# Loading the first inputs in other pieces, turning `gate_w` on TensorE, and warm-up products on constants

## The chip, the cores and the metric

The kernel runs on one core of one Trainium2 chip. The metric is the device time of one execution in microseconds (us); lower is better. Several executions of the kernel before were timed, and one execution was recorded by the hardware profiler; all durations of single instructions below come from that one recorded execution.

## The reference

With x of 2048 tokens by 512 features, the reference adds two branches, mixed token by token by a gate:

```python
g = sigmoid((x * gate_w).sum(-1, keepdims=True))      # one number per token
a = A(x, wq, wk, wv, wo, beta)                        # attention in 4 segments of 512 tokens, 32 heads of 16
b = (gelu(x @ w_gate) * (x @ w_up)) @ w_down          # 1792 hidden features
out = g * a + (1 - g) * b
```

`A` is causal softmax attention inside each segment of 512 tokens, mixed per head (by `sigmoid(beta)`) with a linear-attention memory that is carried from segment to segment, and then a product with `wo`. All inputs and the output are bf16.

## The kernel before

**Layout.** A segment's x is held transposed, features on partitions: `xS[s]` is 128 partitions by 4 feature blocks (`fc`) by 512 tokens. K and Q are computed transposed (`u_k`, `u_q`: four products of 128 by 128 by 512 accumulate over `fc` in one PSUM bank, then a copy, called a cast in this text, brings them to SBUF). V is computed with tokens on partitions (`u_v`, four products of 448 columns for each of four token blocks `kt`). The last 64 columns of V and the gate's sum, `x @ gate_w`, come together in `u_vz` (tile `zT`): `gate_w` is kept as a further column, number 512, of the tile `wv`. `u_vz` reads columns 448 to 512, `u_v` reads columns 0 to 447.

**The start.** Everything is emitted in program order, engine by engine, and each engine runs its own list in that order. `load_inputs` (L134) issues seven transfers on SP's queue: x of segment 0 (into `x0`, which borrows the tile `G[1]`), `wk`, `wq`, `beta`, `wv`, `gate_w`, and `wga` (the weights of the gelu branch's gate product, 1.8 MB). x of segment 0 comes in as it lies in memory, 128 tokens by 512 features for each of four blocks, so every piece that one transfer row moves has 1 KB. Meanwhile `warm_up` (L155) clears a piece of `G[1]` on VectorE and runs six products of 512 columns and sixteen small ones on it; their results are not used. `transpose_x0` (L169) then turns x on TensorE, 16 products in four groups of four, one group per feature block, and VectorE and ScalarE copy the groups alternately to `xS[0]`. Then come, in this order on TensorE: three K blocks (`u_k(0, c)` for c below 3, tile `kT`), four Q blocks (`qT`), four V blocks (`vT`), `u_vz` (`zT`), and fourteen gate blocks (`u_gate`, tile `gT`, L440), which need `wga`. Between Q and V, `load_rest` (L143) has VectorE write a few elements of `xS[1]`; the transfer of x of segment 1 waits for that, and the other large weights (`wup`, `wdn`, `wo`) follow it in SP's queue.

**PSUM.** The tiles of the start (`warm`, `x0T`, `kT`, `qT`, `vT`, `zT`, `gT`) all take turns in the same four banks, tag `gen`. A tile can be written when the tile four before it has been read out.

**The rest.** After the fourteenth gate block a list scheduler, run when the program is built, has fixed one order of instructions for attention (`lg`, `pT`, `od`), memory, gate, up, down and output products of all four segments. It works with estimated costs (`MM512`, `EVAC`, `EXP_T` and so on) and does not look at the start, so this order is the same whatever the start does.

Of the kernel before, what the change touches and what calls it, by code (L numbers as in the profile page):

```python
# [13 lines left out]
P = 128  # L14
D = 512
# [3 lines left out]
DFF = 1792  # L19
FC = D // P  # L20
# [11 lines left out]
BF = dt.bfloat16  # L32
# [21 lines left out]
def kernel(  # L54
# [15 lines left out]
    nc = tc.nc  # L70
    S = A_x.shape[1]
    L = S // NSEG
    KT = L // P
    assert A_x.shape[0] == 1 and A_x.shape[2] == D and L == 512 and KT == 4
    x2 = A_x[0]
# [6 lines left out]
    pgen = ctx.enter_context(tc.tile_pool(name="pgen", bufs=4, space=bass.MemoryType.PSUM))  # L82

    def const(shape, dtype, name):
        return cpool.tile(shape, dtype, name=name, tag=name)

    xS = [const([P, FC, L], BF, f"x{i}") for i in range(NX)]
    wq = const([P, FC, D], BF, "wq")
    wk = const([P, FC, D], BF, "wk")
    wv = const([P, FC, D + 2], BF, "wv")  # L90
    wo = const([P, FC, D], BF, "wo")
    wup = const([P, FC, DFF], BF, "wup")
    wga = const([P, FC, DFF], BF, "wga")
    wdn = const([P, HS, D], BF, "wdn")
    ident = const([P, P], BF, "ident")
# [11 lines left out]
    G = [const([P, HS, L], BF, f"G{i}") for i in range(NG)]  # L107
# [17 lines left out]
    def gen(name):  # L125
        return pgen.tile([P, 512], F32, name=name, tag="gen")

    def x_seg(s):
        nc.sync.dma_start_transpose(xS[s % NX][:, :, :], x2[s * L:(s + 1) * L, :])

    def cols(dst, src):
        nc.sync.dma_start(dst[:, :, :], src.rearrange("(fc p) n -> p fc n", p=P))

    def load_inputs():  # L134
        nc.sync.dma_start(x0, x2[0:L, :].rearrange("(k p) d -> p k d", p=P))
        cols(wk, A_wk)
        cols(wq, A_wq)
        nc.sync.dma_start(beta[:, :], A_beta.rearrange("(o n) -> o n", o=1).to_broadcast((P, H)))
        cols(wv[:, :, 0:D], A_wv)
        nc.sync.dma_start(wv[:, :, D:D + 1], gate_w.rearrange("(fc p o) -> p fc o", p=P, o=1))  # L140
        cols(wga, B_w_gate)

    def load_rest():  # L143
        nc.vector.memset(xS[1][:, 0, 0:2], 0.0)
        x_seg(1)
        cols(wup, B_w_up)
        x_seg(2)
        cols(wdn, B_w_down)
        cols(wo, A_wo)


    x0 = G[1][:, 0:KT, :]
    zero = G[1][:, KT, :]

    def warm_up():  # L155
        nc.vector.memset(zero, 0.0)
        T = gen("warm")
        for i in range(6):
            nc.tensor.matmul(T[:, :], lhsT=zero[:, 0:P], rhs=zero, start=True, stop=True)

        U = gen("warm")
        for i in range(16):
            j, r = i // 2 % 4, i % 2
            nc.tensor.matmul((T, U)[r][32 * j:32 * j + 32, 0:256],
                             lhsT=zero[64 * r:64 * r + 64, 32 * j:32 * j + 32],
                             rhs=zero[64 * r:64 * r + 64, 0:256], start=True, stop=True,
                             tile_position=(64 * r, 32 * j))

    def transpose_x0():  # L169
        for fc in range(FC):  # L170
            T = pgen.tile([P, 1024], BF, name="x0T", tag="gen")
            for kt in range(KT):
                nc.tensor.transpose(T[:, kt * P:(kt + 1) * P],
                                    x0[:, kt, fc * P:(fc + 1) * P], ident[:, :])
            if fc % 2 == 0:
                nc.vector.tensor_copy(xS[0][:, fc, :], T[:, 0:512])
            else:
                nc.scalar.copy(xS[0][:, fc, :], T[:, 0:512])

    def setup_consts():  # L180
        nc.gpsimd.memset(bm[:, :, :], 1.0)
# [80 lines left out]
    def u_q(s, c):  # L262
        def f():
            T = gen("qT")
            for fc in range(FC):
                nc.tensor.matmul(T[:, :], lhsT=wq[:, fc, c * P:(c + 1) * P],  # L266
                                 rhs=xS[s % NX][:, fc, :],
                                 start=(fc == 0), stop=(fc == FC - 1))
                if fc < FC - 1:
                    yield MM512  # L270
            cast(QT[:, c, :], T[:, :])
            return MM512
        return 4 * MM512, EVAC, f
# [103 lines left out]
    def u_v(s, kt):  # L377
        def f():
            T = gen("vT")
            for fc in range(FC):  # L380
                nc.tensor.matmul(T[:, 0:DV], lhsT=xS[s % NX][:, fc, :][:, kt * P:(kt + 1) * P],  # L381
                                 rhs=wv[:, fc, 0:DV], start=(fc == 0), stop=(fc == FC - 1))
                if fc < FC - 1:
                    yield MM448
            cast(Vh[s % 2][:, kt, :, 0:HV // 2, 0:16].rearrange("q p h d -> q h p d"),
                 T[:, 0:DV].rearrange("q (h p d) -> q h p d", h=HV // 2, p=2))
            return MM448
        return 4 * MM448, EVAC, f
# [261 lines left out]

    ctx.enter_context(tc.manual_schedule())
    load_inputs()
    make_identity(nc, ident[:, :])
    warm_up()
    transpose_x0()
    setup_consts()

# [88 lines left out]
    def run(u):  # L746
        if u[0] == 0.0:
            u[2]()
        else:
            for _ in u[2]():  # L750
                pass
# [3 lines left out]
    for c in range(NC8):  # L755
        run(u_q(0, c))
    load_rest()
    for kt in range(KT):
        run(u_v(0, kt))
    run(u_vz(0))  # L760
# [182 lines left out]
    for pieces in visits:  # L943
# [17 lines left out]
        if lumps and lumps[0][0] == clock[0]:  # L961
            i = lumps.pop(0)[1]
# [5 lines left out]
        n = len(visits) - clock[0]  # L968
# [174 lines left out]
```

## Time and profile before

| | |
|---|---|
| median of 3 runs | 271.45 us (271.13 to 272.18) |
| profiled execution | 270.92 us, of which the span from first to last instruction is 269.2 us |
| TensorE (PE) busy | 262.6 us, 98% of the span |
| first warm-up product | 1.32 us after the start of the span |
| first transposing product | 4.79 us |
| first K product | 6.29 us |
| first gate product | 16.04 us |

Times in the views count from the start of the span. PE is TensorE's products, PEld its weight loads, DVE is VectorE, ACT ScalarE, POOL GpSimd, SP the engine whose queue issues the transfers (SPq is that issuing). A row of the timeline or of the chain gives start, duration, engine, line of the kernel, operation, and output tile `<-` input tiles; in brackets stands how long the engine sat idle before it and what ended that. An `xN` is the number of instructions merged into the row. A row of the windows gives for each engine the busy time in that stretch and the instructions, then the granted TensorE clock, the busy share of the 16 DMA engines, and GB/s. A row of the transfers gives KB and the time from issue to landing.

### The profile page before, as it was taken

The page shows a single profiled execution, that of the slowest core. Times are in us where ns is not written, and L with a number is a line of the kernel's source. Part 1 is how long each engine was busy: PE and PEld are TensorE (multiplying, and loading weights), DVE is VectorE, ACT ScalarE, POOL GpSimd, SP SyncE. Part 2 cuts the span into 40 slices and gives each one's busy share as a digit, 9 for nine tenths or more (in the row PEclk, how much of TensorE's full clock was granted, in tenths as well). Part 3 has the DMA queues.
Part 4 walks back from the last instruction along what each step waited for, and adds up shares of the span by engine and source line. Part 5 has one row for each costly group of instructions (what it writes and reads, how often), then busy time and mean ns, then how long its engine had stood idle before and what let it go on. Part 6 is the DMA issues. An engine that isn't in the chain of part 4 may idle for free.

```text
span 269.2 us, 6568 instructions
## 1 busy us (share of the span) xinstructions
PE 262.6 (98%) x2713; PEld 117.7 (44%) x2713; DVE 203.4 (76%) x390; ACT 208.8 (78%) x163; POOL 156.8 (58%) x298
## 2 busy tenths in 40 slices
PE   7999999999999999999999999999999999999993
PEld 2454434344454444545444444444444544344451
DVE  1899575968778787697986979596888588697374
ACT  3236889999997998889999988889888987567420
POOL 4000158897905979987811998596875079654400
PEclk9999999999999999999999999999999999999998
DMA  6899931200160000301042001100000300003102
GB/s 226 281 223 280 319 86 39 41 4 0 22 142 2 0 22 22 78 2 43 0 62 62 2 21 45 38 29 13 19 23 21 67 2 19 16 5 41 39 22 85
DMA packets 29986, 16.60 MB, mean 62 GB/s; under 512 B 20480, under 2 KB 28928, under 8 KB 29952
## 3 DMA queue, kind: packets, MB, share of 16 engines
q1 hardware_dynamic: 29952, 16.14, 23.6%
q8 instruction: 22, 0.36, 0.6%
q14 instruction: 12, 0.10, 0.1%
HBM read 8.14 MB, written 2.10 MB: 38 GB/s over the span
## 4 chain that ended last, share of the span: by engine, by line
PE 86%; POOL 5%; issue 4%; DMA 2%; ACT 1%; DVE 0%; SPq 0%; ACTq 0%; DVEq 0%; POOLq 0%
PE gT L440 19%; PE uT L461 17%; PE dT L477 14%; PE lg L602 8%; PE od L627 6%; PE aT L494 5%; PE qT L266 5%; PE kT L352 5%; PE vT L381 4%; POOL pT L611 3%; POOL KTm L362 2%; DMA wk<-in_A_wk_dram 2%; PE MT L515 1%; PE mn L584 1%; ACT pT L607 1%
## 5 line engine op out<-in xcount | busy, mean ns | idle before, releaser
L611 POOL TENSOR_SCALAR_AFFINE_SELECT pT<-pT 64x256 bf16<-64x256 bf16 x256 | 113.8, 445 | 94.6 <-ACT pT L607 81.7
L607 ACT ACTIVATE pT<-lg 128x2048 bf16<-128x2048 f32 x72 | 135.1, 1876 | 24.9 <-PE lg L602 21.6
L461 PE MATMUL uT<-x,wup 128*128 128x512 bf16 x224 | 60.4, 380 | 0.0
L440 PE MATMUL gT<-x,wga 128*128 128x512 bf16 x224 | 57.0, 380 | 0.0
L477 PE MATMUL dT<-wdn,G 128*128 128x512 bf16 x224 | 52.9, 380 | 0.0
L467 DVE TENSOR_TENSOR G<-uT,G 128x512 bf16<-128x512 f32 x56 | 38.1, 684 | 6.4 <-PE uT L461 6.2
L362 POOL TENSOR_SCALAR KTm<-ktb,eo 128x512 bf16<-128x512 bf16 x26 | 40.6, 1571 | 1.3
L634 DVE STREAM_TRANSPOSE oq<-od 128x512 f32<-128x512 f32 x32 | 21.0, 695 | 19.5 <-PE od L627 19.5
L477 PEld LDWEIGHTS <-G 128*128 128x128 bf16 x224 | 20.8, 98 | 25.0 <-issue 2.1
L440 PEld LDWEIGHTS <-wga 128*128 128x128 bf16 x224 | 20.4, 98 | 24.0 <-issue 2.2
L461 PEld LDWEIGHTS <-wup 128*128 128x128 bf16 x224 | 19.8, 98 | 24.0 <-issue 5.4
L602 PE MATMUL lg<-QT,KTm 32*128 32x192 bf16 (+7 forms) x512 | 28.6, 287 | 0.0
L289 DVE CAST G<-gT 128x512 bf16<-128x512 f32 x24 | 16.5, 688 | 9.9 <-PE gT L440 9.7
L602 PEld LDWEIGHTS <-KTm 32*128 32x128 bf16 x512 | 8.3, 92 | 28.4 <-issue 28.0
L627 PE MATMUL od<-pT,V 64*32 64x128 bf16 (+7 forms) x512 | 19.4, 284 | 0.2 <-POOL pT L611 0.2
L627 PE MATMUL od<-pT,Vs 64*32 64x128 bf16 (+7 forms) x512 | 19.4, 284 | 0.0
L455 ACT ACTIVATE G<-G 128x3584 bf16<-128x3584 bf16 x6 | 18.8, 3182 | 0.0
L640 DVE SCALAR_TENSOR_TENSOR o<-oq,ogs,rden 128x256 bf16<-128x256 f32 x32 | 17.0, 532 | 1.1
L352 PE MATMUL kT<-x,wk 128*128 128x512 bf16 x64 | 16.8, 380 | 0.4 <-DMA wk<-in_A_wk_dram 0.4
L266 PE MATMUL qT<-x,wq 128*128 128x512 bf16 x64 | 16.6, 379 | 0.0
L499 DVE SCALAR_TENSOR_TENSOR tB<-aT,gct,tB 128x512 bf16<-128x512 f32 x16 | 11.9, 746 | 6.0 <-PE aT L494 5.7
L494 PE MATMUL aT<-wo,oT 128*128 128x512 bf16 x64 | 16.5, 380 | 0.0
(94 smaller groups left out, 274.5 us busy)
## 6 DMA issues: line engine op xcount, KB each, us to landing
out_dram<-tB SPq DMA_DIRECT2D x16, 128.0 KB, 1.7
wga<-in_B_w_gate_dram SPq DMA_DIRECT2D x1, 1792.0 KB, 12.0
wup<-in_B_w_up_dram SPq DMA_DIRECT2D x1, 1792.0 KB, 9.9
wdn<-in_B_w_down_dram SPq DMA_DIRECT2D x1, 1792.0 KB, 8.0
Vs<-V SPq DMA_DIRECT2D x8, 144.0 KB, 2.6
G<-in_A_x_dram SPq DMA_DIRECT2D x1, 512.0 KB, 4.0
wk<-in_A_wk_dram SPq DMA_DIRECT2D x1, 512.0 KB, 4.9
wq<-in_A_wq_dram SPq DMA_DIRECT2D x1, 512.0 KB, 5.8
```

Source lines behind the costliest of these rows:

```text
L266: nc.tensor.matmul(T[:, :], lhsT=wq[:, fc, c * P:(c + 1) * P], rhs=xS[s % NX][:, fc, :], start=(fc == 0), stop=(fc == FC - 1))
L352: nc.tensor.matmul(T[:, :], lhsT=wk[:, fc, c * P:(c + 1) * P], rhs=xS[s % NX][:, fc, :], start=(fc == 0), stop=(fc == FC - 1))
L362: eng.tensor_scalar(out=KTm[:, (NC8 * s + c) % NK, :, p, :], in0=ktb[:, c, :].rearrange("q (b k) -> q b k", b=NB), scalar1=eo[:, p:p + 1], ...
L440: nc.tensor.matmul(T[:, :], lhsT=wga[:, fc, hs * P:(hs + 1) * P], rhs=xS[s % NX][:, fc, :], start=(fc == 0), stop=(fc == FC - 1))
L461: nc.tensor.matmul(T[:, :], lhsT=wup[:, fc, hs * P:(hs + 1) * P], rhs=xS[s % NX][:, fc, :], start=(fc == 0), stop=(fc == FC - 1))
L467: nc.vector.tensor_tensor(out=g, in0=T[:, :], in1=g, op=ALU.mult)
L477: nc.tensor.matmul(T[:, :], lhsT=G[s % NG][:, hs, qt * P:(qt + 1) * P], rhs=wdn[:, hs, :], start=(hs == 0), stop=(hs == HS - 1))
L494: nc.tensor.matmul(T[:, :], lhsT=oT[:, fc, qt * P:(qt + 1) * P], rhs=wo[:, fc, :], start=(fc == 0), stop=(fc == FC - 1))
L602: nc.tensor.matmul(lg[:, j, off:off + n], lhsT=KTm[rows, i % NK, b].rearrange("r p k -> r (p k)"), rhs=QT[rows, i % NC8, 64 * b:L], start= ...
L607: nc.scalar.activation(pT[:, :, :], lg[:, :, :], AF.Exp, scale=DH ** -0.5)
L611: nc.gpsimd.affine_select(out=v, in_=v, pattern=[[0, 4], [1, 64]], compare_op=ALU.is_ge, fill=0.0, base=0, channel_multiplier=-1)
L627: nc.tensor.matmul(od[p][32 * j:32 * j + 32, 64 * b:L], lhsT=w[:, 18 * h:18 * h + 32], rhs=t[rows, j, off:off + n], start=(b == 0), stop=( ...
```

## The change

x of segment 0 is loaded in two transfers of 256 tokens. In each of them a partition takes two neighbouring tokens, 2 KB in one piece; the transposed copy then puts token 2p+k of the half to its place, so that its writes step over every second element. `transpose_x0` goes half by half, each half in two groups that hold two feature blocks; VectorE copies the first group of each half, ScalarE the second. `wk` comes in two transfers of 256 columns, so its pieces are 512 bytes. `gate_w` comes as four rows of 128 elements into a corner of `G[1]`; a product with the identity turns them between Q and V (`transpose_gw`, in a PSUM bank of its own), and VectorE writes column 512 of `wv` from it. `beta` is issued after `wv`. `wga` comes in two transfers, 512 columns and 1280 columns. The warm-up products read constants that the preamble has set, one of them repeated by a step of zero, so the clearing on VectorE goes; five large products remain of six.

```diff
     def load_inputs():
-        nc.sync.dma_start(x0, x2[0:L, :].rearrange("(k p) d -> p k d", p=P))
-        cols(wk, A_wk)
+        half = L // 2
+        for i in range(2):
+            nc.sync.dma_start(x0[:, 2 * i:2 * i + 2, :],
+                              x2[half * i:half * (i + 1), :].rearrange("(p k) d -> p k d", p=P))
+        for i in range(2):
+            n = slice(D // 2 * i, D // 2 * (i + 1))
+            cols(wk[:, :, n], A_wk[:, n])
         cols(wq, A_wq)
+        nc.sync.dma_start(gw4, gate_w.rearrange("(fc p) -> fc p", p=P))
+        cols(wv[:, :, 0:D], A_wv)
         nc.sync.dma_start(beta[:, :], A_beta.rearrange("(o n) -> o n", o=1).to_broadcast((P, H)))
-        cols(wv[:, :, 0:D], A_wv)
-        nc.sync.dma_start(wv[:, :, D:D + 1], gate_w.rearrange("(fc p o) -> p fc o", p=P, o=1))
-        cols(wga, B_w_gate)
+        for n in (slice(0, 4 * P), slice(4 * P, DFF)):
+            cols(wga[:, :, n], B_w_gate[:, n])
...
     x0 = G[1][:, 0:KT, :]
-    zero = G[1][:, KT, :]
+    gw4 = G[1][0:FC, KT, 0:P]
 
     def warm_up():
-        nc.vector.memset(zero, 0.0)
         T = gen("warm")
-        for i in range(6):
-            nc.tensor.matmul(T[:, :], lhsT=zero[:, 0:P], rhs=zero, start=True, stop=True)
+        for i in range(5):
+            nc.tensor.matmul(T[:, :], lhsT=nc.const_aps.tensor(1.0, [P, P], BF),
+                             rhs=nc.const_aps.tensor(1.0, [P, 512], BF), start=True, stop=True)
...
             nc.tensor.matmul((T, U)[r][32 * j:32 * j + 32, 0:256],
-                             lhsT=zero[64 * r:64 * r + 64, 32 * j:32 * j + 32],
-                             rhs=zero[64 * r:64 * r + 64, 0:256], start=True, stop=True,
-                             tile_position=(64 * r, 32 * j))
+                             lhsT=nc.const_aps.tensor(1.0, [64, 32], BF, 64 * r),
+                             rhs=nc.const_aps.tensor(1.0, [64, 256], BF, 64 * r),
+                             start=True, stop=True, tile_position=(64 * r, 32 * j))
 
     def transpose_x0():
-        for fc in range(FC):
-            T = pgen.tile([P, 1024], BF, name="x0T", tag="gen")
-            for kt in range(KT):
-                nc.tensor.transpose(T[:, kt * P:(kt + 1) * P],
-                                    x0[:, kt, fc * P:(fc + 1) * P], ident[:, :])
-            if fc % 2 == 0:
-                nc.vector.tensor_copy(xS[0][:, fc, :], T[:, 0:512])
-            else:
-                nc.scalar.copy(xS[0][:, fc, :], T[:, 0:512])
+        for half in range(2):
+            for f0 in range(0, FC, 2):
+                T = pgen.tile([P, 1024], BF, name="x0T", tag="gen")
+                for i in range(4):
+                    fc, k = f0 + i // 2, i % 2
+                    nc.tensor.transpose(T[:, i * P:(i + 1) * P],
+                                        x0[:, 2 * half + k, fc * P:(fc + 1) * P], ident[:, :])
+                dst = xS[0][:, f0:f0 + 2, half * 256:half * 256 + 256].rearrange(
+                    "q f (p k) -> q f k p", k=2)
+                src = T[:, 0:512].rearrange("q (f k p) -> q f k p", f=2, k=2)
+                if f0 == 0:
+                    nc.vector.tensor_copy(dst, src)
+                else:
+                    nc.scalar.copy(dst, src)
+
+    def transpose_gw():
+        T = pgen.tile([P, 1024], BF, name="gwT", tag="gen")
+        nc.tensor.transpose(T[:, 0:FC], gw4, ident[0:FC, 0:FC])
+        nc.vector.tensor_copy(wv[:, :, D], T[:, 0:FC])
...
     load_rest()
+    transpose_gw()
     for kt in range(KT):
         run(u_v(0, kt))
```

## The prediction

> **What bounds the kernel now.** The page's first and fourth parts say which engine sets the time.
>
> ```profile
> PE 262.6 (98%) x2713; PEld 117.7 (44%) x2713; DVE 203.4 (76%) x390; ACT 208.8 (78%) x163; POOL 156.8 (58%) x298
> PE 86%; POOL 5%; issue 4%; DMA 2%; ACT 1%; DVE 0%; SPq 0%; ACTq 0%; DVEq 0%; POOLq 0%
> ```
>
> PE works 262.6 of 269.2 us. So only what moves PE's work as a whole can move the end, and the change touches nothing behind the start. The chain in order of time shows the start (start, duration, what), and the waits of PE the one wait in it.
>
> ```profile
> 1.31 4.94 DMA wk<-in_A_wk_dram
> 6.29 2.76 PE kT L352 x12
> 9.06 3.45 PE qT L266 x16
> 12.51 3.03 PE vT L381 x16
> 15.54 0.48 PE zT L397 x16
> 16.04 12.26 PE gT L440 x56
> 30.46 0.86 PE uT L461 x4
> ```
> ```profile
> PE kT L352 <- DMA wk<-in_A_wk_dram: 0.4, 1, 0.4
> ```
>
> The chain begins with the transfer of `wk`. From 6.29 us PE runs without a wait through K, Q, V, z and gate, and after that the order is fixed. If the first K product comes earlier by d and nothing behind it becomes late, the end comes earlier by d. What could become late is seen in the transfers (KB, us from issue to landing) and their issues.
>
> ```profile
> G<-in_A_x_dram SPq DMA_DIRECT2D x1, 512.0 KB, 4.0
> wk<-in_A_wk_dram SPq DMA_DIRECT2D x1, 512.0 KB, 4.9
> wq<-in_A_wq_dram SPq DMA_DIRECT2D x1, 512.0 KB, 5.8
> wv<-in_A_wv_dram SPq DMA_DIRECT2D x1, 512.0 KB, 8.0
> wv<-in_gate_w_dram SPq DMA_DIRECT2D x1, 1.0 KB, 8.0
> wga<-in_B_w_gate_dram SPq DMA_DIRECT2D x1, 1792.0 KB, 12.0
> wup<-in_B_w_up_dram SPq DMA_DIRECT2D x1, 1792.0 KB, 9.9
> ```
> ```profile
> 0.79 0.47 SPq L135 DMA_DIRECT2D G<-in_A_x_dram  x1
> 1.31 0.49 SPq L132 DMA_DIRECT2D wk<-in_A_wk_dram  x1
> 1.85 0.50 SPq L132 DMA_DIRECT2D wq<-in_A_wq_dram  x1
> 3.98 1.29 SPq L132 DMA_DIRECT2D wga<-in_B_w_gate_dram  x1
> 15.99 0.57 SPq L132 DMA_DIRECT2D wup<-in_B_w_up_dram  x1
> ```
>
> Issue plus time to landing: x 4.8, `wk` 6.2, `wq` 7.65, `wga` 15.98, `wup` 25.9 us. `wga` lands 0.06 us before its first product: without new pieces an earlier K would only wait there. `wup` has 4.6 us to spare.
>
> **The change part by part.** *Rates.* Windows (stretch, length, busy time of PE, PEld, DVE, ACT, POOL, then granted clock, DMA share, GB/s) give the speed of the transfers; the last one, late in the kernel, holds `Vs` transfers, whose rows have 576 bytes.
>
> ```profile
> 2.20:2.40 0.20, 0.20 (x2) 0.10 (x1) 0.00 (x0) 0.00 (x0) 0.20 (x2) 1.00 0.59 148
> 3.40:3.90 0.50, 0.50 (x2) 0.00 (x0) 0.00 (x0) 0.00 (x0) 0.35 (x1) 1.00 1.09 383
> 7.40:7.90 0.50, 0.50 (x4) 0.27 (x3) 0.50 (x1) 0.00 (x0) 0.00 (x0) 1.00 0.56 195
> 12.00:13.00 1.00, 1.00 (x7) 0.49 (x6) 1.00 (x3) 0.00 (x0) 0.00 (x0) 1.00 1.02 419
> 213.80:214.40 0.60, 0.60 (x4) 0.29 (x3) 0.00 (x0) 0.60 (x1) 0.00 (x0) 1.00 0.96 216
> ```
>
> Rows of 1 KB run at 383 GB/s, rows of 3.5 KB at 419, rows of 576 bytes at 216 (from SBUF, so this is a lower bound for `wk` in 512). At its start x runs at only 148.
>
> *x in halves.* The second half of x is the last byte of the same 512 KB. Latest: it lands at 4.8 as now. Earliest: if the slow start is a cost per row, half as many rows save about half of a slow microsecond, 4.3. I take 4.6, nearer to the unchanged rate; the first half then lands one half (262 KB at 383 GB/s, 0.68 us) earlier, at 3.9.
>
> ```profile
> 1.32 2.74 PE L159 MATMUL warm<-G 128*128 128x512 bf16 x6 [1.32 <-DVE G L156]
> 3.99 0.56 PE L164 MATMUL warm<-G 64*32 64x256 bf16 x16
> 4.79 1.07 PE L173 MATMUL x0T<-ident,G 128*128 128x128 bf16 x16 [0.24 <-DMA G<-in_A_x_dram]
> 5.23 0.87 DVE L176 COPY x<-x0T 128x512 bf16<-128x512 bf16 x2 [3.96 <-PE x0T L173]
> 5.45 1.07 ACT L178 COPY x<-x0T 128x512 bf16<-128x512 bf16 x2 [3.31 <-PE x0T L173]
> ```
> ```profile
> L176 DVE COPY x<-x0T x2: 425/425/425, 5.2 to 5.7; 128x512 bf16<-128x512 bf16 x2
> L289 DVE CAST QT<-qT x4: 682/682/684, 11.1 to 12.9; 128x512 bf16<-128x512 f32 x4
> ```
>
> From the first transposing product to the first copy pass 0.44 us (4.79 to 5.23). The copy took 0.425 us with dense writes; the new one writes every second element, which no row shows. It is bounded below by 0.425 and above by the 0.68 us of a cast of as many elements; I take the upper end. After the second half lands only two groups are left: 4.6 + 0.44 + 0.68 = 5.72. ScalarE's copy starts 0.22 later and takes half of 1.07, or 5.8; it is needed by the third K product only, 0.43 behind the first.
>
> *wk in halves.* Its first half follows x: 0.68 us at 383 GB/s, 1.21 at 216. So it lands at 5.3 to 5.8; I take 5.6. Before, all of `wk` was waited for until 6.25. K starts at the later of the two, **5.75** instead of 6.29: 0.54 us earlier. The ends: 4.3 + 0.44 + 0.43 = 5.2, rounded up to 5.3 for semaphores; and 4.8 + 1.21 = 6.0.
>
> One page of the Trainium skill speaks against this part: "DMA: Bandwidth & Descriptors", section "Rules for kernel authors", wants small transfers merged into one large one, and its specifications put the line rate at 512 bytes and above. Taken alone, the first rule would leave no gain from halves; the second would put `wk` at the fast end. The trace's 216 GB/s at 576 bytes agrees with the first more than with the second, and no row here has 512 bytes from HBM.
>
> *What comes behind K.* The second half of `wk` lands by 7.0 and is needed 8 products of 0.216 later than K's start, at 7.5. `wq` landed 1.4 after `wk`: 8.4 at the latest of my values, needed at 5.75 + (9.06 - 6.29) = 8.5. So this is close, and with all transfers at their slow end it decides (rival below). `beta` and `gate_w` lie ahead of `wga` now, and the window at 7.4 shows 195 GB/s at share 0.56 there: moving `beta` behind `wv` and making `gate_w` four rows takes small rows out of the way. `wv` then lands between 9 and 11.5 and is needed at 12.0. `wga`'s first 512 columns land at 13 at the latest (`wga` took 5.0 us behind `wv`, and they are 2/7 of it), needed at 15.5; the rest needs no more than before, 15.98, and is needed 16 products later, at 19. Three more issues at 0.5 us on SP are covered: the transfers run several us behind their issues. The transfers of `load_rest` wait for VectorE's write and move with it.
>
> *gate_w's product.* It is one short product on PE, 0.06 us, and it takes a turn in the four banks: V's first block must now wait for the second Q cast instead of the first. The casts begin at 11.13 and 0.6 apart, so that one ends at 12.41, and V starts in the chain at 12.51. Both move with K. I put the product and the tighter turn at 0.1 us (0.05 to 0.15). VectorE's copy of four elements is a row like this:
>
> ```profile
> 16.51 0.15 DVE L410 COPY gct<-zT 128x4 f32<-128x4 f32 x1
> ```
>
> It stands behind the fourth Q cast (ends 13.6) and is wanted by V's fourth block, at 14.8; if V's first block had to wait for it, because column 512 of `wv` were not told from columns 0 to 447, it would cost 1.3 us. In the program before, V's products wait for `wv`'s transfer and only z's for `gate_w`'s, so I count nothing.
>
> *Warm-up.* Without VectorE's clearing, PE starts at about 1.0 instead of 1.32; five products of 0.42 and the sixteen small ones end at about 3.7, just ahead of x's first half. This moves nothing on the chain as long as the later products run at full speed.
>
> ```profile
> L159 PE MATMUL warm<-G x6: 606/634/635, 1.3 to 3.4; 128*128 128x512 bf16 x6
> L164 PE MATMUL warm<-G x16: 354/378/393, 4.0 to 4.2; 64*32 64x256 bf16 x16
> L173 PE MATMUL x0T<-ident,G x16: 219/219/229, 4.8 to 5.6; 128*128 128x128 bf16 x16
> ```
>
> The large warm-up products stand 0.42 us apart, K's 0.216: PE began at half speed, although the granted clock reads 1.00. A small product of 256 columns still took 0.38 at 4.0; the transposing ones stand 0.057 apart from 4.79 on, full speed. So PE opened between 4.2 and 4.8, that is 2.9 to 3.5 us after its first product, after 3.2 us of nearly unbroken work.
>
> *Sum.* Against the profiled execution: 270.92 - 0.54 + 0.10 = 270.48. The median of the runs stands 0.53 above that execution, so 271.45 - 0.44 = **271.0 us**. From the ends (0.24 and 1.0, less 0.1) its own range is 270.5 to 271.4.
>
> **The rivals.** *PE is still at half speed when K comes* (slower). The work ahead of K shrinks from 3.2 us without a pause and 1.07 to 2.7 us and two groups of eight with pauses around them. If this no longer opens PE, the count begins again at K: 2.9 to 3.5 us at half speed from 5.75, half of it lost, 1.45 to 1.75, and about 0.2 for the half-speed products ahead of the last copies. With the gain of 0.44 taken off, +1.2 to +1.5: 272.8. The point that decides is whether PE opens before about 6 us. For it: the trace shows an opening only after 3.2 us of work. Against it: transposing at half speed fills the pauses. "TensorE: Matmul & The Clock Gate" of the Trainium skill, Part 1, says that activity is judged in a free-running window of about 3.4 us, which would make this a matter of chance in each run; the opening 2.9 to 3.5 us after the first product agrees. Its Part 4 adds that transposing products do not count as busy in the same way, which by that rule would let the pause from 3.7 to 5.75 count whole and give the same 272.8.
>
> *The start gains more than the chain shows* (faster). If the slow start of x is a cost per row, K starts at 5.3, 0.9 net. And the runs of 271.13 to 272.18 beside a profiled 270.92 may hold waits that this trace lacks, `wga`, with 0.06 us to spare, first of all. If the change removes that 0.53 too: 271.45 - 0.9 - 0.53 = 270.0.
>
> *The halves come no earlier* (the change does not do what it says). Rows of 512 bytes at 216 GB/s and x at its old rate: K at 6.05, less 0.1, and `wq` at its limit: 271.3.
>
> **How the numbers follow.** Forecast 0.48, half speed 0.22, more than the chain 0.18, no earlier 0.12. A difference under 0.5% (1.36 us) is about what a measurement of this kernel can tell from no change; faster means below 270.09, slower above 272.81. Of the half-speed case, at 272.65 to 272.95 before the runs' scatter, three quarters count as slower: 0.17. Of the faster rival two thirds, 0.12, and of the forecast's scatter 0.07: 0.19. The rest is 0.64. The range runs from the faster rival's 270.0 to the middle of the half-speed case, 272.8; it leaves out about 0.09 below and 0.11 above.
>
> **What would show it.** K's first product at 5.3 to 6.05, released by VectorE's copy or by `wk`; no wait of PE from there to the gate beyond 0.1 us, none on `wga`; K's products 0.216 apart; warm-up from 1.0 to 3.7; the strided copy between 0.43 and 0.68 us; the span shorter by what K moved, less 0.1. K products 0.43 apart show the slow rival; a wait on `wq` of 0.2 us or more, or V behind the copy of `gate_w`, shows a step of the sum wrong.

## The result, and the profile after

The changed kernel takes 270.78 us (median of 13 runs, 270.49 to 271.17), the kernel before 271.6 us (13 runs beside them, 270.65 to 272.83). The ratio is 0.9972, 95% interval 0.9959 to 0.9985: 0.4 to 1.1 us less. The runs lie within 0.7 us of each other, those before within 2.2. The profiled execution took 270.57 us with a span of 268.8, against 270.92 and 269.2.

First the chain of the changed kernel in order of time (start, duration, what), and the waits of PE and of its weight loads in the first 30 us.

```profile
1.71 4.07 DMA wk<-in_A_wk_dram
5.83 2.76 PE kT L368 x12
8.59 3.54 PE qT L282 x16
12.13 0.11 PE gwT L193
12.23 3.13 PE vT L397 x16
15.37 0.48 PE zT L413 x16
15.85 12.09 PE gT L456 x56
```
```profile
PE kT L368 <- DMA wk<-in_A_wk_dram: 0.9, 1, 0.9
PEld L282 <- DMA wq<-in_A_wq_dram: 0.4, 1, 0.4
```

In this execution K starts 0.46 us earlier and still waits for `wk`, now for its first half. The first Q weights have a new wait, for `wq`. Next PE's timeline, first of the changed kernel, then of the one before.

```profile
0.97 2.31 PE L164 MATMUL warm<-const-bfloat16-1.0 128*128 128x512 bf16 x5 [0.97 <-PEq L1144]
3.77 1.15 PE L181 MATMUL x0T<-ident,G 128*128 128x128 bf16 x16
5.83 2.76 PE L368 MATMUL kT<-x,wk 128*128 128x512 bf16 x12 [0.91 <-DMA wk<-in_A_wk_dram]
8.50 3.63 PE L282 MATMUL qT<-x,wq 128*128 128x512 bf16 x16
12.17 3.20 PE L397 MATMUL vT<-wv,x 128*128 128x448 bf16 x16
15.21 0.64 PE L413 MATMUL zT<-wv,x 128*128 128x65 bf16 x16
15.69 0.81 PE L456 MATMUL gT<-x,wga 128*128 128x512 bf16 x3
```
```profile
8.89 3.62 PE L266 MATMUL qT<-x,wq 128*128 128x512 bf16 x16
12.35 3.19 PE L381 MATMUL vT<-wv,x 128*128 128x448 bf16 x16
15.38 0.65 PE L397 MATMUL zT<-wv,x 128*128 128x65 bf16 x16
16.04 1.25 PE L440 MATMUL gT<-x,wga 128*128 128x512 bf16 x5
```

Taking first starts from stage to stage:

| from to | before | after | difference |
|---|---|---|---|
| start to K | 6.29 | 5.83 | -0.46 |
| K to Q | 2.60 | 2.67 | +0.07 |
| Q to V | 3.46 | 3.67 | +0.21 |
| V to z | 3.03 | 3.04 | +0.01 |
| z to gate | 0.66 | 0.48 | -0.18 |

The sum is -0.35 us, the whole difference of the two profiled executions. The last line is the one to learn from: before, the sixteen z products were followed by a gap that the list of waits did not show, because `wga` landed at 15.98 and z ended at about the same time. With `wga` there in time the step takes 0.48 us.

The medians differ by 0.82, not 0.35. The experiments ask where the rest is. Two theories: **P** (pieces), the runs of the kernel before wait for `wga` at the first gate product, more in some than in the profiled one; **O** (opening), PE leaves half speed at a moment that differs from run to run, and the earlier warm-up brings it forward. "PE opens" means here that it leaves half speed: K's products of 512 columns stand 0.43 us apart before and 0.216 after.

### The profile page after: what moved, and what is told of

Its sections match the earlier page's. It is cut to its first block, busy times and chain, and to the rows that moved or that the text cites. A ratio compares the mean times of both kernels' runs of the same rounds, so it can differ in the third digit from the quotient of the medians.

```text
span 268.8 us, 6576 instructions
## 1 busy us (share of the span) xinstructions
PE 262.3 (98%) x2713; PEld 117.5 (44%) x2713; DVE 203.7 (76%) x390; ACT 209.0 (78%) x163; POOL 156.8 (58%) x298
## 4 chain that ended last, share of the span: by engine, by line
PE 86%; POOL 5%; issue 4%; DMA 2%; ACT 1%; SPq 0%; DVE 0%; ACTq 0%; DVEq 0%; POOLq 0%
PE gT L456 19%; PE uT L477 17%; PE dT L493 14%; PE lg L618 8%; PE od L643 6%; PE aT L510 5%; PE qT L282 5%; PE kT L368 5%; PE vT L397 4%; POOL pT L627 3%; POOL KTm L378 2%; DMA wk<-in_A_wk_dram 2%; PE MT L531 1%; PE mn L600 1%; ACT pT L623 1%
```

## The experiments

The median of the kernel before, run beside each group, was 271.3 us for e1 to e4 (270.65 to 272.7), 271.65 for e5, e6, e8 and e9 (270.61 to 272.66), and 271.15 for e7 and e10 (270.8 to 272.79). So medians of different groups are compared by their ratios to the kernel before; each ratio below has its 95% interval behind it.

### e1: the gate weights in two transfers, nothing else

```diff
-        cols(wga, B_w_gate)
+        for n in (slice(0, 4 * P), slice(4 * P, DFF)):
+            cols(wga[:, :, n], B_w_gate[:, n])
```

> The kernel before with the gate weights in two transfers and nothing else changed. Theory P (pieces: the gain is K's earlier start plus a wait of the first gate product on wga that varies from run to run): the first gate product starts 0.18 us earlier against z, span 269.0, median 0.2 to 0.6 us lower, and the runs lie closer together. Theory O (opening: the chance of when PE leaves half speed makes the runs before differ by 2 us, and the earlier warm-up narrows that): at most 0.2 us lower, runs as far apart as before.

Measured: 271.11 us, 270.65 to 271.42, ratio 0.9992 (0.998 to 1.0004). The median fell by 0.2, which the interval does not tell from nothing. But no run of twelve is above 271.42, while of the kernel before's 35 runs 14 are: the long runs went with the one edit that touches only `wga`. That is what P expects. z to gate takes 0.48 (15.62 to 16.10).

### The kernel before, once more, for its trace

> The kernel before once more, for its trace: half of its runs take over 271.6 us. If this execution is one of them: by theory P its first gate product waits 0.5 us or more for wga behind z, and K's products stand 0.216 apart; by theory O K's products are at half speed (12 in over 3.3 us) and the gate does not wait. If it is a short one: z to gate under 0.7 us.

> The kernel before a third time, with the same readings: in an execution over 271.6 us, theory P has the first gate product wait 0.5 us or more for wga with K at full speed, theory O has K's 12 products take over 3.3 us and no wait at the gate.

The first of the two executions took 271.96 us, a long one, the second 270.96. PE's timeline and wait of the long one:

```profile
6.27 2.55 PE L352 MATMUL kT<-x,wk 128*128 128x512 bf16 x11 [0.37 <-DVE eo L188]
15.38 0.65 PE L397 MATMUL zT<-wv,x 128*128 128x65 bf16 x16
16.98 1.25 PE L440 MATMUL gT<-x,wga 128*128 128x512 bf16 x4 [0.95 <-DMA wga<-in_B_w_gate_dram]
```
```profile
PE gT L440 <- DMA wga<-in_B_w_gate_dram: 0.9, 1, 0.9
```

K runs at full speed (11 recorded products in 2.55), z starts exactly where it did in the first profile, and the gate starts 0.94 us later, at 16.98, waiting for `wga`. The span is 0.9 us longer than in the first profile, which is this wait. In the short execution the listed wait on `wga` is 0.24. Counted as in the table, from the first z product to the first gate product, the three traces of the kernel before hold 0.66 us (the first profile), 0.88 (15.19 to 16.07, the short one) and 1.60 (15.38 to 16.98, the long one), where 0.48 is enough: a wait of 0.18, 0.40 and 1.12 us. So P is shown for a long run. How much each of the other long runs waited is not recorded.

### e2: the new warm-up alone; e9: the same with `wga` in two

e2 is the kernel before with the new `warm_up` of the diff; e9 adds e1's edit.

> The kernel before with the warm-up of the changed kernel (five products on the preamble's constants, from about 0.97 us) and nothing else. Theory P: no difference, within 0.1 us, runs as far apart as before. Theory O: median 0.4 us lower and all runs within 1 us.

> The kernel before with the warm-up on constants (as in e2) and wga in two transfers (as in e1). Theory O: the long runs of e2 come from K at half speed after the pause of 0.9 us between warm-up and x; they stay, median 271.7 to 272.1, K's 12 products take up to 4.5 us. Theory P: they come from wga landing late; with wga in two they go, median 271.1, all runs within 0.8 us.

Measured: e2 272.15 us (270.84 to 272.95), ratio 1.0022 (1.0004 to 1.004); e9 272.25 us (271.64 to 272.91), ratio 1.0025 (1.0008 to 1.0042). Both theories were wrong on e2, and O has the right mechanism with the other sign. The first two rows are e2's, the last is e9's.

```profile
4.75 1.89 PE L173 MATMUL x0T<-ident,G 128*128 128x128 bf16 x16 [0.91 <-DMA G<-in_A_x_dram]
6.42 4.71 PE L352 MATMUL kT<-x,wk 128*128 128x512 bf16 x12
```
```profile
6.46 3.94 PE L353 MATMUL kT<-x,wk 128*128 128x512 bf16 x12
```

The new warm-up ends at 3.84 and x, still in one transfer, lands at 4.75. After that pause of 0.9 us the transposing products take 1.89 instead of 1.07, and K's twelve 4.71 or 3.94 instead of 2.76: PE is still at half speed well into K. (The column of the granted clock reads 1.00 all through K in e2 and e9; half speed is read from the products here.) The slow transposing products alone are no sign of the pause, since e4, whose start is that of the kernel before, has 1.89 too; slow K products are. The changed kernel has the same warm-up without the pause, and its K products are at full speed. e9 against e1, which differ in the warm-up alone, is 1.14 us of median, or 0.9 by the ratios (1.0025 against 0.9992). So the earlier warm-up does not pay without an earlier x.

### e3: x and wk in halves alone

e3 is the kernel before with the first two loops of the new `load_inputs` and the new `transpose_x0`.

> The kernel before with x and wk in halves and x in rows of 2 KB; wga, beta, gate_w and warm-up as before. Theory P: K starts at 5.8 us instead of 6.29, but the first gate product waits for wga and starts where it did, 16.0 or later; span and median as before within 0.2 us. If wga does not bind, the whole 0.46 us shows and the median is 0.4 to 0.5 lower. Theory O: the same as P for the median, runs 2 us apart.

Measured: 271.43 us, 271.11 to 271.75, ratio 1.0 (0.9986 to 1.0013). The time was right, the reason was not:

```profile
4.55 1.89 PE L180 MATMUL x0T<-ident,G 128*128 128x128 bf16 x16
6.83 2.73 PE L362 MATMUL kT<-x,wk 128*128 128x512 bf16 x11 [0.39 <-DVE x L186]
```

K starts at 6.83, not 5.8. The old warm-up holds PE until 4.55, so the half of x that landed at about 3.6 (issue at 0.8, 2.8 to landing) waits, and then all sixteen transposing products run at half speed, which e4's do as well; K waits for VectorE's copy. `wga` does not bind here (wanted at 16.57, landed at 15.9), and the runs lie within 0.7 us. Neither half of the new start, e2 or e3, gains alone. Both together without the other edits were not run; what they give in the changed kernel is estimated further below, under "What the parts give".

### e4: gate_w as rows with its product, and beta behind wv

```diff
+        nc.sync.dma_start(gw4, gate_w.rearrange("(fc p) -> fc p", p=P))
+        cols(wv[:, :, 0:D], A_wv)
         nc.sync.dma_start(beta[:, :], ...)
-        cols(wv[:, :, 0:D], A_wv)
-        nc.sync.dma_start(wv[:, :, D:D + 1], gate_w.rearrange("(fc p o) -> p fc o", p=P, o=1))
...
     load_rest()
+    transpose_gw()
```

> The kernel before with gate_w as four rows and its product between Q and V, and beta behind wv; all else as before. Theory P: from the first Q product to the first V product 0.2 us more (bank turn and product), wga lands at least 0.3 us earlier so that the first gate product no longer waits (0.18 back); net 0.0 to 0.1 us and runs closer together. Theory O: 0.2 us slower, runs as far apart as before.

Measured: 271.0 us, 270.83 to 271.43, ratio 0.9983 (0.9968 to 0.9998); the runs are close together as P said. The same two windows of the kernel before and of e4 (the last two columns are the DMA share and GB/s) show what the small rows held up:

```profile
7.00:8.00 1.00, 1.00 (x6) 0.44 (x5) 0.63 (x1) 0.00 (x0) 0.00 (x0) 1.00 0.52 161
9.00:10.00 1.00, 1.00 (x7) 0.42 (x5) 0.96 (x4) 0.69 (x2) 0.00 (x0) 1.00 0.61 167
```
```profile
7.00:8.00 1.00, 1.00 (x6) 0.46 (x5) 0.33 (x1) 0.21 (x1) 0.00 (x0) 1.00 1.07 356
9.00:10.00 1.00, 0.95 (x5) 0.47 (x5) 0.96 (x4) 0.00 (x0) 0.00 (x0) 1.00 0.82 291
```

Between the two, from 8 to 9 us, the kernels are alike (202 and 215 GB/s). Which of the two edits, `beta` or `gate_w`, gives how much is not separated. `wga` lands a microsecond earlier, at 14.9, and z to gate takes 0.48 here too (15.89 to 16.37). Q to V takes 3.65 (9.20 to 12.85), the 0.2 us of the new product.

### e5: the changed kernel with wga in one transfer

e5 takes e1's edit back out of the changed kernel.

> The changed kernel with the gate weights in one transfer again. If two parts of wga matter once the small rows are out of the way: the first gate product, now wanted at 15.7, waits for wga, 0.1 to 0.5 us, and the median is 270.9 to 271.3 with runs further apart. If they no longer matter, because x, wk, gate_w and beta already let wga land by 15.3: no wait on wga, median as the changed kernel, 270.8, runs within 0.8 us.

Measured: 270.83 us, 270.32 to 272.69, ratio 0.9985 (0.9966 to 1.0005). The second case for the median: z to gate is 0.48 (15.36 to 15.84). But two of twelve runs, 271.41 and 272.69, lie above everything that the changed kernel gave in 13. They fit a late `wga`, which in the profiled execution landed at about 15.8, hardly ahead of its use; no trace of the two exists, so this is not shown.

This trace shows one more thing. Up to K, e5 and e6 (described below, as e10 is) have the same start as the changed kernel, and in e10 only the order of the transfers behind `wq` differs. The transposing products start at 3.77 us in the changed kernel's profile and within 0.01 us of that in these three, but they take 1.73 (e5), 1.89 (e6) and 1.77 us (e10) instead of 1.15: they are at half speed for most of the time, and K starts later. e6's rows:

```profile
3.77 1.89 PE L181 MATMUL x0T<-ident,G 128*128 128x128 bf16 x16
6.05 2.79 PE L368 MATMUL kT<-x,wk 128*128 128x512 bf16 x12 [0.39 <-DVE x L187]
```

So O's premise holds: the moment when PE opens differs between executions of the same start. K's first product in the four traces of the changed start stands at 5.83, 6.07 (e5), 6.05 (e6) and 6.04 (e10), 6.00 on average. In the five traces of the start before it stands at 6.29, 6.27 and 6.11 (the kernel before), 6.36 (e1) and 6.38 (e4), 6.28 on average. The 0.46 of the table is thus the early end; 0.28 is the difference of the averages.

### e6 and e10: what gate_w's product costs

e6 runs `transpose_gw()` behind the second V block; e10 has no product and loads `gate_w` element by element between the parts of `wga`:

```diff
+        cols(wga[:, :, 0:4 * P], B_w_gate[:, 0:4 * P])
+        nc.sync.dma_start(wv[:, :, D:D + 1], gate_w.rearrange("(fc p o) -> p fc o", p=P, o=1))
+        cols(wga[:, :, 4 * P:], B_w_gate[:, 4 * P:])
```

> The changed kernel with the product of gate_w between the second and third V block instead of ahead of the first. Theory B (bank): V's first block waits for the second Q cast because of the extra turn; moved, the first V product comes 0.15 to 0.2 us earlier against the first Q product (3.46 instead of 3.67), median 270.6. Rival: the 0.2 us has another cause (PE's product itself, or the casts), and nothing changes.

> The changed kernel with gate_w again as 512 elements, but issued between the two parts of wga, and without its product on PE. If the product with its weight load costs PE 0.2 us whatever its place (e6): Q's first product to z's first 0.2 us shorter, median 270.55 to 270.65. If gate_w then lands too late for z (wanted at 15.0): z waits and the median is 271 or more.

Measured: e6 270.88 us (270.67 to 271.15), ratio 0.9974 (0.9958 to 0.999); e10 270.63 us (270.32 to 271.22), ratio 0.9977 (0.9962 to 0.9992). PE's timeline, e6 first:

```profile
12.12 1.68 PE L397 MATMUL vT<-wv,x 128*128 128x448 bf16 x8
13.73 0.17 PE L193 MATMUL gwT<-ident,G 4*128 4x4 bf16 x1
13.84 1.69 PE L397 MATMUL vT<-wv,x 128*128 128x448 bf16 x8
```
```profile
8.65 3.63 PE L282 MATMUL qT<-x,wq 128*128 128x512 bf16 x15
12.11 3.19 PE L397 MATMUL vT<-wv,x 128*128 128x448 bf16 x16
15.14 0.64 PE L413 MATMUL zT<-wv,x 128*128 128x65 bf16 x16
```

`gwT` has no bank of its own; like the other tiles of the start it takes a turn in the four of tag `gen`, which is why the bank was suspected. In e6 Q to V is back at 3.45 (8.67 to 12.12), but V to z is 3.24 instead of 3.03: the 0.2 us moved with the product. So the bank theory falls; the product takes the 0.2 us wherever it stands. Without it (e10) Q to z takes 6.49 against 6.71. Its median is 0.15 below the changed kernel's, which these runs cannot tell apart; its K started at 6.04, released by VectorE's copy.

### e7: the changed kernel with wk in one transfer

```diff
-        for i in range(2):
-            n = slice(D // 2 * i, D // 2 * (i + 1))
-            cols(wk[:, :, n], A_wk[:, n])
+        cols(wk, A_wk)
```

> The changed kernel with wk in one transfer (rows of 1 KB). If wk's halves carry the earlier start: K waits for the whole of wk until 5.9 to 6.2, 0.1 to 0.4 us later, median 270.9 to 271.2. If x alone carries it, or the 512-byte rows cost as much as the half saves (wq lands earlier with 1 KB rows and Q no longer waits): median 270.7 to 270.8.

Measured: 273.94 us, 271.38 to 275.2, ratio 1.0092 (1.0062 to 1.0122). Far outside both expectations.

```profile
3.77 1.24 PE L179 MATMUL x0T<-ident,G 128*128 128x128 bf16 x16
7.37 4.38 PE L366 MATMUL kT<-x,wk 128*128 128x512 bf16 x12 [2.36 <-DMA wk<-in_A_wk_dram]
```
```profile
5.50:6.00 0.50, 0.00 (x0) 0.00 (x0) 0.16 (x3) 0.27 (x1) 0.00 (x0) 1.00 0.43 127
7.00:7.50 0.50, 0.13 (x1) 0.13 (x2) 0.00 (x0) 0.00 (x0) 0.00 (x0) 0.76 1.09 378
7.50:8.00 0.50, 0.50 (x2) 0.15 (x1) 0.00 (x0) 0.00 (x0) 0.00 (x0) 0.50 1.07 377
```

PE was at full speed in the transposing products (1.24 for 16), then idle for 2.36 us, and K ran at half speed: the granted clock, third from the end, reads 0.76 and 0.50. So full speed was lost in this pause; `wk`'s first half keeps the pause of the changed kernel at 0.91. From the readings 0.76 for 7.0 to 7.5 and 0.83 for 10.5 to 11.0 the half speed lasted from about 7.26 to 10.67, 3.4 us. Of the 3.2 us that this kernel's median lies above the changed one's, the later K explains about 1.5 (7.37 against 5.83) and the half speed about 1.6 (4.38 against 2.76). e7 does not tell whether the pause counts from the transposing products, 2.36 us, or from the end of the warm-up at 3.84, 3.5 us, which it would be if transposing products did not count as work. Why the whole `wk` landed only at 7.3, when the transfers ran at 127 GB/s and share 0.43 in between, is open.

### e8: the changed kernel without warm-up products

> The changed kernel without any warm-up product. Theory O: PE stays at half speed through the transposing products and most of K and Q; first Q product 2 us or more later than in the changed kernel, median 272.2 to 273.0, runs 1 us or more apart. Rival: the transposing products open PE by themselves before K, median within 0.3 us of the changed kernel.

Measured: 271.45 us, 271.12 to 272.58, ratio 1.0003 (0.9983 to 1.0022). This is O's mechanism at less than half of its price:

```profile
3.66 1.89 PE L181 MATMUL x0T<-ident,G 128*128 128x128 bf16 x16 [3.66 <-DMA G<-in_A_x_dram]
6.17 3.81 PE L368 MATMUL kT<-x,wk 128*128 128x512 bf16 x12 [0.63 <-DMA wk<-in_A_wk_dram]
```

K's twelve products take 3.81 instead of 2.76, so PE opened within K. The warm-up is worth 0.7 us of the median (0.8 by the ratios).

## Why the prediction was right, point by point

The forecast was 271.0 us, range 270.0 to 272.8; measured 270.78. The direction and the place are right. That the number is so near is in part luck: several terms of the sum were mis-sized, and they offset each other. K's earlier start was taken too large, and a wait for `wga` that the sum put at nothing made up for it.

- **x in halves**: taken at 4.6 for the second half, earliest 4.3. It landed earlier than that:

```profile
G<-in_A_x_dram SPq DMA_DIRECT2D x2, 256.0 KB, 2.8
wk<-in_A_wk_dram SPq DMA_DIRECT2D x2, 256.0 KB, 4.2
wq<-in_A_wq_dram SPq DMA_DIRECT2D x1, 512.0 KB, 5.7
```
```profile
2.50:3.00 0.50, 0.50 (x2) 0.00 (x0) 0.00 (x0) 0.00 (x0) 0.50 (x4) 1.00 1.02 373
5.00:5.50 0.50, 0.00 (x0) 0.00 (x0) 0.50 (x2) 0.50 (x2) 0.00 (x0) 1.00 0.96 282
```

  The second half is issued at 1.25 and takes about 2.8, so 4.05. From 2.5 to 3.0 us the transfers of the changed kernel move 373 GB/s and those of the kernel before 248. But in the prediction's first window, 2.2 to 2.4, the changed kernel moves only 61 GB/s against 148. So x comes sooner; that the slow start was a cost per row, the faster rival's premise, is not shown, since the new x differs in the number of transfers as well.
- **wk in halves**: taken at 5.6, landed at 5.78. Its 512-byte rows run at 282 GB/s in the second window, between the bounds 216 and 383. So K waits for `wk` in this trace, not for the copy: 5.83 against 5.75, 0.46 instead of 0.54. In e6 and e10 it waits for the copy, and over the traces K gains 0.28. "DMA: Bandwidth & Descriptors" of the Trainium skill, section "Rules for kernel authors", wants small transfers merged; with `wk` in one transfer K started at 7.37 (e7), so merging did not pay here, though the slow stretch in e7 is unexplained.
- **The copy** with every second element:

```profile
L187 DVE COPY x<-x0T x2: 710/722/733, 4.3 to 4.9; 128x512 bf16<-128x512 bf16 x2
```

  0.72 us, just above the upper bound that was taken, 0.68.
- **wq** landed at 2.73 + 5.7 = 8.4, the latest value given; it cost Q 0.07. The prediction wanted it at 8.5, from the chain's 9.06 for Q; the timeline has Q's first product at 8.89, so it was wanted at about 8.35, and the small wait could have been seen.
- **gate_w's product** with its turn in the banks was put at 0.1 and came to 0.2, and e6 shows that the bank is not the reason.
- **wga** was the step that failed in its reading: "0.06 us before its first product" was called no wait. z to gate held 0.18 us of wait in that very trace, and 1.12 in another (p1). The rival "the start gains more than the chain shows" named this and gave it 0.53. p1 shows it in one long run, and the long runs went in e1; how much of the difference between -0.35 for the profiled executions and -0.82 for the medians it carries is not shown. The median of the kernel before alone moved between 271.15 and 271.65 from group to group.
- **PE at half speed**, the slower rival, did not reach K in any of the four traces of the changed start. It did reach the transposing products in three of them (e5, e6, e10), and the 0.2 us that the rival counted ahead of the last copies is what those traces show: K at 6.04 to 6.07 instead of 5.83. K itself was at half speed in e2, e9, e7 and e8; the price, put at 1.65 to 1.95 before the gain, was 1.14 between e9 and e1. The prediction's second way of counting, by which transposing products are no work and the pause before K counts whole (3.84 to 5.83), did not come true: K ran at full speed. "TensorE: Matmul & The Clock Gate" of the Trainium skill, Part 1, makes the opening a matter of a free-running window of about 3.4 us; the transposing products of one and the same start, 1.15 to 1.89 us, agree with chance from run to run, and the 3.4 us of half speed in e7 agrees with the length.
- **What the parts give.** e4 alone has the ratio 0.9983, the changed kernel 0.9972. The difference, 0.3 us, would be the share of the new start (x, `wk` and warm-up); it is an estimate and has the size of K's earlier start, 0.28, but the two intervals overlap, so the medians do not show it.

## What to carry to other kernels

A transfer that lands within a tenth of a microsecond of its use, as `wga` did here, can be a wait already, in other runs more than in the profiled one: compare the step with the same step in a trace where the data are early, and look at how far the runs lie apart. Start-up edits come in sets: here an earlier warm-up without earlier data cost 0.9 us and earlier data without the earlier warm-up gave nothing, so judge them together. One trace of a start is one draw: K's start moved by 0.24 us between traces of the same start, half of the gain that the first pair of traces showed. Where the engine must stay at full speed, split the first transfer so that no pause like e7's is left.

## What the runs showed of the hardware that was not expected

- After 1.24 us of transposing products at full speed a pause of 2.36 us put PE back to half speed for 3.4 us (e7, granted clock 0.50), while pauses of 0.39 to 0.91 did not (the four traces of the changed start).
- The moment when PE opens differs between executions of the same start: its sixteen transposing products took 1.15, 1.73, 1.77 and 1.89 us.
- A product of 4 by 128 by 4 in a stream of large ones cost 0.2 us at both places (before V in the changed kernel, within V in e6), and leaving it out gave 0.2 back (e10), though its own row says 0.17 and overlaps its neighbours.
- With 128 short rows of `beta` and 512 elements of `gate_w` ahead of `wga` the transfers moved 161 to 202 GB/s between 7 and 10 us; with `gate_w` in four rows and `beta` behind `wv` they moved 215 to 356, and `wga` landed 1 us earlier (e4).
